# The high half of q copied within SBUF instead of a second evacuation of PSUM

## The chip, the core and the metric

The kernel runs on one core of a Trainium2 chip. The metric is the device time of one execution in microseconds (us), the median of several runs. The engines are TensorE (PE, matmuls; PEld is its weight load), VectorE (DVE), ScalarE (ACT), GpSimd (POOL) and the queue of SyncE (SP), which issues the DMAs.

## The reference

Attention with a bucket mask, then two feed-forward layers. Cut to what matters:

```python
batch, n_heads, seq, head_dim = 2, 8, 768, 64

q_bits = einsum(q, proj) > 0;  k_bits = einsum(k, proj) > 0      # 6 bits each
mask   = bucket(q_bits)[:, None] == bucket(k_bits)[None, :]
scores = where(mask, q @ k.T / sqrt(64), -1e9)
attn   = exp(scores - max(scores)); attn /= sum(attn) + 1e-9
x      = attn @ v                                   # (1536, 512)

h = x @ w_in;   x = (h * tanh(softplus(h))) @ w_out                      # 512 -> 2048 -> 512
h = x @ w_in2;  x = (layernorm(h * softmax(h)) * g_ln) @ w_out2           # 512 -> 1024 -> 512
```

All of it is computed to float32's precision: each factor is split into a high part that TensorE takes exactly and a low rest, and a product is the sum of high times high, high times low and low times high.

## The kernel before

The 16 heads are worked on as 8 pairs. A head has 6 tiles of 128 queries against all 768 keys, so there are 96 tiles. For each tile TensorE makes the scores (line 1238, two operands A and B), VectorE the row maximum (line 1245) and two small steps (lines 1249, 1250), ScalarE the exponential (line 1254). The exponentials are transposed, either as two halves through a DMA (high half by ScalarE, line 1265, low half by GpSimd, line 1287, DMA at line 1290) or by TensorE (line 1273) with halves taken out by ScalarE (line 1277) and VectorE (line 1282). Then TensorE weighs v with them (lines 1305 to 1307), and VectorE divides (lines 1315 to 1319).

Before its tiles, a pair is prepared. GpSimd splits q and k (lines 1137, 1142). TensorE transposes each head's q and k so that the high part lies in 64 partitions and the rest in the other 64 (line 1163, into two PSUM banks called st). ScalarE takes these banks into the operand A (line 1180, 128x768, q scaled by 1/8). The second operand B needs q's high part once more: VectorE reads the same two banks again (line 1171, 64x768, the same scale). k's half of B is copied from A by a DMA (line 1192). Below them, in 12 more rows of B, come the sign bits of q and k (lines 1204, 1212, and the DMA of line 1220), so that one more product adds the mask to the scores.

The first feed-forward layer follows in 48 units of 12 matmuls up (lines 835 to 837) and 12 down (lines 891 to 896), with the function between on ScalarE, VectorE and GpSimd (lines 851 to 877); its weights, 48 chunks, are turned from 64-bit to 32-bit numbers and split on the way (lines 728 to 747). The second layer and its layer norm are 12 tiles at the end (lines 940 to 1029).

Nothing of the order is written out by hand. The class Order holds every step with its engine, its cost in us (COST), its reads and writes, and its due time, which is the number of its tile plus an offset from the table PHASE. Its function run plays the program through with these costs: on each engine it takes, among the steps that can start within 0.1 us of the earliest, the one whose due time is least. What comes out is the order of the instructions on every engine. PSUM's 8 banks and the buffers in SBUF are given out by the same function.

The steps that the change touches have these names there: turn (transposes), evac n h 0 and evac n h 1 (q and k into A), evac n h 2 (q's high part into B). evac="AAAA" gives the first two to ScalarE, again="VV" the third to VectorE for both heads of a pair.

Of the kernel before, what the change touches and what calls it, by code (L numbers as in the profile page):

```python
# [9 lines left out]
F32 = mybir.dt.float32  # L10
# [19 lines left out]


PHASE = dict(
    score=2.89, max=21.69, bias=-20.48, exp=-7.37, hi=37.60, lo=-74.88, tdma=47.79, tr0=9.51, thi0=14.05,
    tlo0=2.17, tr1=10.84, thi1=28.04, tlo1=16.57, weigh=17.46, norm0=29.45, norm1=6.67, norm2=-77.92,
    load=19.06, vload=18.96, split0=-188.88, rest0=28.62, split1=-216.02, rest1=37.27, turn=-44.19,
    evac=-204.06, copy=-27.06, bits0=-103.88, bits1=-136.11, sign=51.37, bdma=40.93, vmax=21.86, vs0=-271.50,
    vs1=9.08, vs2=-210.73, vs3=-129.45, vs4=-56.64, vs5=-127.12, vs6=-290.81, vs7=144.62, vs8=-328.13,
    vh=70.16, vl=45.25, first=63.48, turn_=6.48, evac_=195.41, copy_=-35.91, bits_=94.54, sign_=168.35,
    bdma_=-9.06, vload_=-304.47, vmax_=171.56, vs_=87.04, vh_=-22.87, vl_=-122.68, second=35.58, wload=28.78,
    w0=-41.17, w1=84.02, w2=-26.10, w3=26.15, w4=31.29, w5=19.05, w6=290.37, wpace=-25.50, wat=214.24,  # L40
    wlate=-420.19, turngap=-246.21, x0_=-6.98, x1_=-173.02, x2_=44.49, load_=10.81, const0=66.52,
    begin0=-146.26, vs8_=150.21, outlag=-5.17, up=-162.02, a0=-14.23, a1=40.52, a2=25.54, a3=14.48, a4=30.07,
    a5=-71.43, a6=11.38, a7=-135.40, a8=-17.97, a9=76.71, a10=229.81, da=51.52, db=-112.61, ky0=101.10,
    ky1=110.82, x0=37.16, x1=118.52, x2=72.93, sy0=21.03, sy1=8.66, u2=24.00, n0=-198.44, n1=78.28, n2=130.92,
    n3=-69.22, n4=-178.31, n5=-31.52, n6=140.09, n7=224.60, n8=-279.51, n9=-111.63, n10=-196.61, n11=-61.38,
    n12=-275.68, n13=3.09, t2=-8.41, l0=-92.90, l1=222.42, d2=202.96, ot=-141.26, od=-47.76, wloadL=-156.21,
    w0L=2.89, w1L=23.01, w2L=229.21, w3L=-26.73, w4L=229.00, w5L=-89.36, w6L=-69.41, begin1=-117.25,
    begin2=-102.32, begin3=76.98, const1=123.70, const3=67.06, load0_=-1.00,
)


COST = dict(
    score=0.79, max=0.865, bias=0.18, exp=0.878, hiA=0.733, hiD=0.469, lo=1.61, tr=0.33, thi=0.371, tlo=0.469,
    weigh=0.555, norm0=0.075, norm1=0.106, norm2=0.531, split=0.8, rest=1.79, turn=0.515,
    evacA=0.691, evacV=0.865, warm=3.2, bits=0.7, sign=0.985, vmax=0.87, vs0=0.11, vs1=0.2, vs2=0.11,
    vs=0.07, vs8=0.884, vh=0.733, firstA=0.413, firstD=0.469, w0=0.56, w1=0.602, w2=0.602,
    w3=0.602, w4=0.783, w5=0.52, w6P=1.253, w6D=0.663, x0=0.47, x1=0.478, x2=0.602,
    up=0.7, a0=0.494, a1=0.335, a2=0.602, a3=0.613, a4=0.52, a9=0.52, a10=1.25, da=0.464, db=0.2265,
    sy0=0.52, sy1=0.602, u2=1.39, n0=1.131, n1=1.091, n2=0.069, n3=0.075, n4=1.196, n5=0.069, n6=1.133,
# [17 lines left out]
class Order:  # L77


    def __init__(self, rings, stores, slack, due):  # L80
        self.rings, self.stores, self.slack, self.due = rings, stores, slack, due
        self.kinds = {kind: (name, n) for name, (size, kinds) in stores.items() for kind, n in kinds.items()}
        self.ops, self.index, self.writer, self.readers, self.users = [], {}, {}, {}, {}
        self.spare = dict(e=2, p16=1)

    def op(self, key, engine, cost, base, name, reads=(), writes=(), slot=0, behind=(), wait=()):
        i = len(self.ops)
# [28 lines left out]
    def shared(self, o):  # L116

        key, engine = o[0], o[1]
        if engine == "Pool":
            return True  # L120
        if engine != "DVE":
            return False
        k = key[0]
        if k in ("hi", "sy", "mg"):
            return True
        if k == "first":
            return True
        if k == "w":
            return key[2] == 6
        if k == "n2":  # L130
            return key[3 - 1] == 13
        return False
# [5 lines left out]
    def run(self):  # L138
# [64 lines left out]
        for _ in range(n):  # L203
            best = None
            for e, line in queue.items():
                cand = []
                for r, i in line:
                    r = max(r, free[e])
                    if ops[i][7]:
                        r = ring(i, r)[0]  # L210
                        if r is None:
                            continue
                    cand.append((r, due[i], i))
                if not cand:
                    continue
                first = min(cand)[0]
                pick = min((c for c in cand if c[0] <= first + self.slack), key=lambda c: c[1:])
                if best is None or pick[0] < best[0]:
                    best = (pick[0], e, pick[2])
            at, e, i = best  # L220
            o = ops[i]
            queue[e] = [x for x in queue[e] if x[1] != i]
            for tok, name, m, k in ring(i, at)[1]:
                place[tok] = k
                held[name][k:k + m] = [tok] * m
            for tok in o[7]:
                if tok[0] in taken:
                    taken[tok[0]].append(tok)
            start[i] = at
            if o[8] is not None:  # L230
                hw = max(at + 0.05, hw) + o[2]
                begin = max(hw + 0.65, wire)
                wire = done[i] = begin + o[8]
                if e == "SP":
                    free[e] = begin + 0.85 if o[0][0] in ("tdma", "td") else hw
                else:
                    free[e] = at + 0.05
            else:
                if shared[i]:
                    at = start[i] = max(at, port[other[e]])  # L240
                    port[e] = at + o[2]
                free[e] = done[i] = at + o[2] * (2 if e == "PE" and at < COLD and o[0][0] != "warm" else 1)
            got.append(i)
            for tok in o[10]:
                busy[tok] -= 1
                was = idle.setdefault(tok, {})
                was[frm[i]] = max(was.get(frm[i], 0.0), done[i])
            for j in then[i]:
                left[j] -= 1
                if not left[j]:  # L250
                    queue[ops[j][1]].append((ready(j), j))
# [19 lines left out]
def program_order(pairs, tiles, routes, evac, chunks, wide, due, rings, stores, slack, queues=(), pooled=0,  # L271
# [3 lines left out]
    op = order.op  # L275
# [30 lines left out]
    def prep(n):  # L306
# [6 lines left out]
        for h in range(2):  # L313
            th = t0 if n else h * due["second"]
            for o in range(2):
                sp = ("sp%d" % o, n) if n else ("f", o, h)
                if not n:
                    op(("first", 0, h, o), A, COST["firstA"], th, "first", [(("r%d", "rr%d")[h] % o, 0)], [sp], 0,
                       [("evac", 0, 0, 1)] if h else [])
                    op(("first", 1, h, o), V, COST["firstD"], th, "first", [(("r%d", "rr%d")[h] % o, 0)], [sp])  # L320
                s = ("st", n, h, o)
                d = t0 + (2 * h + o) * due["turngap"] if n else th + 0.01 * o
                op(("turn", n, h, o), T, COST["turn"], d, "turn" + f, [sp, ("ident",)],
                   [s, ("A%d" % o, n, h)])
                e = evac[2 * h + o]
                op(("evac", n, h, o), A if e == "A" else V, COST["evac" + e], d, "evac" + f, [s], [("A%d" % o, n, h)])
                if again and (o if n == 0 else not o):
                    g = again[h]
                    op(("evac", n, h, 2), A if g == "A" else V, COST["evac" + g], d, "evac" + f, [("st", n, h, 0)],
                       [("B", n, h, 0)])  # L330
            for o in range(1 if again else 0, 2):
                dma(("copy", n, h, o), th + 2 * h, "copy" + f, [("A%d" % o, n, h)], [("B", n, h, o)])
            if not n:
                bits(n, (h,), th, f)
# [256 lines left out]
def lsh_attention_moe_kernel(  # L591
# [33 lines left out]
    queues=(),  # L625
    pooled=48,
    split="G",
    again="VV",
    soon=4,
    by_dma=10,  # L630
):
# [533 lines left out]
    def qk_again(p, h):  # L1165
        dst = second(p, h, 0)[0:64].rearrange("p (a n) -> p a n", a=2)
        src = two_banks("st", p, h, 0)[0:64, :, 0:NH]
        if again[h] == "A":
            nc.scalar.activation(dst, src, AF.Copy, scale=SC)
        else:  # L1170
            nc.vector.tensor_scalar(dst, src, SC, None, op0=ALU.mult)
# [244 lines left out]
```

## Time and profile before

| | us |
|---|---|
| median of 3 runs | 654.56 (653.5 to 655.46) |
| profiled execution | 653.04 |
| its span, first to last instruction | 651.3 |
| TensorE busy | 622.2 (96%) |
| VectorE busy | 558.7 (86%) |
| ScalarE busy | 444.0 (68%) |
| GpSimd busy | 367.5 (56%) |

The busy times are sums over the whole span, over stages that have little in common: attention's last weighing matmul is at 247 us, the first layer's last matmul up at 503 us. Matmuls are pipelined and their ends are modelled, so that a busy TensorE is not TensorE at its peak.

### The profile page before, as it was taken

The numbers are of one execution on the slowest core, as the hardware profiler recorded it, in microseconds if no ns is written. First come the engines' busy times: TensorE is split into PE (matmuls) and PEld (weight loads), VectorE is DVE, ScalarE is ACT, GpSimd is POOL, SyncE is SP. The second block draws the span as 40 slices with busy tenths as digits, with TensorE's granted clock in tenths as the row PEclk, the third lists the DMA queues.
The fourth block names the chain that finished last, engine by engine and source line by source line (L and its number), as shares of the span: only waits on it lengthen the run. The fifth ranks groups of instructions, "written<-read, shape, count | busy, mean of one in ns | idle before, by whom it ended". The sixth has DMA issues, their size and how long they took to land.

```text
span 651.3 us, 12308 instructions
## 1 busy us (share of the span) xinstructions
PE 622.2 (96%) x4460; PEld 513.1 (79%) x4460; DVE 558.7 (86%) x1149; ACT 444.0 (68%) x722; POOL 367.5 (56%) x301
## 2 busy tenths in 40 slices
PE   7889999999899899999999999999999999999997
PEld 6668787888778788878888777788788888788885
DVE  4899798898989999999999999999999776675652
ACT  5689897998999986766565566656566545565543
POOL 4678868777765675566666666455476421222210
PEclk9799899999999999999999999999999999999999
DMA  7979978989898892312333322212121022322221
GB/s 203 219 166 148 243 162 159 170 212 166 180 186 165 151 205 76 97 50 79 98 98 97 98 97 66 94 61 70 35 97 34 1 64 45 81 71 81 66 64 49
DMA packets 146909, 73.36 MB, mean 113 GB/s; under 512 B 125344, under 2 KB 139808, under 8 KB 146848
## 3 DMA queue, kind: packets, MB, share of 16 engines
q1 hardware_dynamic: 146848, 72.58, 47.5%
q8 instruction: 35, 0.57, 0.4%
q14 instruction: 26, 0.21, 0.1%
HBM read 34.68 MB, written 3.15 MB: 58 GB/s over the span
## 4 chain that ended last, share of the span: by engine, by line
PE 42%; DVE 22%; ACT 6%; issue 5%; DMA 1%; POOL 0%; DVEq 0%; ACTq 0%; SPq 0%
PE banks L835 4%; PE banks L837 3%; PE banks L940 3%; PE banks L836 3%; PE banks L944 3%; PE banks L941 3%; PE banks L896 3%; PE banks L891 3%; PE banks L892 3%; PE banks L1029 3%; PE banks L1027 3%; DVE mx L1245 3%; PE banks L1028 3%; DVE a L865 2%; DVE a L853 2%
## 5 line engine op out<-in xcount | busy, mean ns | idle before, releaser
L1287 POOL TENSOR_TENSOR store<-store 128x768 f16<-128x768 f32 x64 | 104.9, 1651 | 48.6 <-ACT store L1265 44.3
L1254 ACT ACTIVATE store<-banks,mx 128x768 f32<-128x768 f32 x96 | 92.4, 998 | 12.3 <-DVE mx L1250 5.0
L1245 DVE TENSOR_REDUCE mx<-banks 128x1 f32<-128x768 f32 x96 | 89.4, 946 | 3.1 <-PE banks L1238 2.0
L869 POOL TENSOR_TENSOR n<-c,a 128x512 f32<-128x512 f32 x48 | 63.8, 1329 | 44.6 <-DVE a L865 42.3
L877 POOL TENSOR_TENSOR gl<-n,gh 128x512 fp32r<-128x512 f32 x48 | 62.9, 1310 | 33.4 <-ACT gh L874 33.0
L835 PE MATMUL banks<-xh,w 128*128 128x512 f32 x192 | 76.6, 399 | 2.5 <-DVE a L865 1.6
L891 PE MATMUL banks<-gh,w 128*128 128x512 f32 x192 | 75.8, 395 | 0.9 <-ACT gh L874 0.8
L837 PE MATMUL banks<-xh,w 128*128 128x512 f32 x192 | 75.7, 394 | 0.0
L836 PE MATMUL banks<-xl,w 128*128 128x512 f32 x192 | 75.4, 393 | 0.0
L892 PE MATMUL banks<-gh,w 128*128 128x512 f32 x192 | 75.3, 392 | 0.0
L859 ACT ACTIVATE a<-n,two 128x512 f32<-128x512 f32 x48 | 34.8, 724 | 56.7 <-DVE n L855 56.4
L896 PE MATMUL banks<-gl,w 128*128 128x512 f32 x192 | 72.4, 394 | 0.0
L743 POOL TENSOR_TENSOR w<-wf,w 128x512 fp32r<-128x512 f32 x40 | 51.7, 1293 | 35.2 <-ACT w L741 33.9
L1238 PE MATMUL banks<-A,A 128*128 128x384 f32 x192 | 58.5, 387 | 8.4 <-ACT store L1254 7.4
L1305 PE MATMUL banks<-v,store 128*128 128x65 f16 x576 | 60.0, 193 | 2.3 <-DVE store L1282 1.9
L1306 PE MATMUL banks<-v,store 128*128 128x64 f16 x576 | 59.8, 194 | 0.0
L1307 PE MATMUL banks<-v,store 128*128 128x65 f16 x576 | 59.6, 192 | 0.0
L1305 PEld LDWEIGHTS <-store 128*128 128x128 f16 x576 | 53.0, 96 | 5.0 <-issue 4.6
L1306 PEld LDWEIGHTS <-store 128*128 128x128 f16 x576 | 53.3, 97 | 2.9 <-issue 2.5
L1265 ACT ACTIVATE store<-store 128x768 f16<-128x768 f32 x64 | 53.3, 849 | 0.2
L1307 PEld LDWEIGHTS <-store 128*128 128x128 f16 x576 | 53.5, 99 | 0.0
L1238 PE MATMUL banks<-B 76*128 76x384 f32 x192 | 51.5, 350 | 0.0
(131 smaller groups left out, 1731.7 us busy)
## 6 DMA issues: line engine op xcount, KB each, us to landing
wr<-in_moe_w_in_dram SPq DMA_DIRECT2D x24, 512.0 KB
wr<-in_moe_w_out_dram SPq DMA_DIRECT2D x24, 512.0 KB
vr<-in_v_dram SPq DMA_DIRECT2D x8, 384.0 KB
B<-A SPq DMA_DIRECT2D x16, 192.0 KB
out_dram<-ot SPq DMA_DIRECT2D x12, 256.0 KB
q<-in_q_dram SPq DMA_DIRECT2D x7, 384.0 KB
k<-in_k_dram SPq DMA_DIRECT2D x7, 384.0 KB
B<-bits SPq DMA_DIRECT2D x32, 36.0 KB
```

What stands on the lines that cost most here:

```text
L835: nc.tensor.matmul(h, lhsT=wh[:, ks], rhs=xh, start=(kk == 0), stop=False)
L836: nc.tensor.matmul(h, lhsT=wh[:, ks], rhs=xl, start=False, stop=False)
L837: nc.tensor.matmul(h, lhsT=wl[:, ks], rhs=xh, start=False, stop=(kk == KD - 1))
L891: nc.tensor.matmul(y, lhsT=wh[:, os], rhs=g_t[u][0], start=first, stop=False)
L892: nc.tensor.matmul(y, lhsT=wl[:, os], rhs=g_t[u][0], start=False, stop=False)
L1238: nc.tensor.matmul(s[:, half, 0:NH], lhsT=opnd[nm, p, j, 0][:, cc], rhs=opnd[nm, p, j, 1][:, hs], start=(i == 0), stop=(i == 1),)
L1245: nc.vector.reduce_max(m[:, 1:2], two_banks("s", t)[:, :, 0:NH], axis=AX.XY, negate=True)
L1254: nc.scalar.activation(kept("e", t).rearrange("p (a n) -> p a n", a=2), two_banks("s", t)[:, :, 0:NH], AF.Exp, bias=m[:, 3:4], scale=m[:, ...
L1287: nc.gpsimd.tensor_tensor(p16[:, 1], kept("e", t), p16[:, 0], op=ALU.subtract)
L1305: nc.tensor.matmul(o, lhsT=pt[:, 0, kc, :], rhs=vh, start=(kc == 0), stop=False)
L1306: nc.tensor.matmul(o[:, 0:D], lhsT=pt[:, 0, kc, :], rhs=vl, start=False, stop=False)
L1307: nc.tensor.matmul(o, lhsT=pt[:, 1, kc, :], rhs=vh, start=False, stop=(kc == NC - 1))
```

## The change

Three things change.

The copy. q's high part comes into B from the operand A, which lies in SBUF and already is scaled, and not from PSUM. Of the two heads of a pair one copy is made by ScalarE (kind a), the other by VectorE (kind v). The copy reads what line 1180 has written; it doesn't read the banks.

The scheduler. It gets a table of partners (other): of two steps that read the same bank it starts neither while the other runs. The table is filled where the second copy is of kind A or V. It also gets a set (port) of VectorE steps that it keeps apart from GpSimd's; the copies of kind v are in it. Two costs are added for the copies, 0.733 us on ScalarE and 0.469 on VectorE.

The table PHASE. All its numbers are new, so the whole program is put in another order.

```diff
 PHASE = dict(
-    score=2.89, max=21.69, bias=-20.48, exp=-7.37, hi=37.60, lo=-74.88, tdma=47.79, tr0=9.51, thi0=14.05,
+    score=2.99, max=78.03, bias=-127.69, exp=-377.90, hi=127.72, lo=-75.93, tdma=195.91, tr0=9.77,
...
-    evacA=0.691, evacV=0.865, warm=3.2, bits=0.7, sign=0.985, vmax=0.87, vs0=0.11, vs1=0.2, vs2=0.11,
+    evacA=0.691, evacV=0.865, evaca=0.733, evacv=0.469, warm=3.2, bits=0.7, sign=0.985, vmax=0.87, vs0=0.11, vs1=0.2, vs2=0.11,
...
+        self.other, self.port = {}, set()
...
-        if k in ("hi", "sy", "mg"):
+        if k in ("hi", "sy", "mg") or key in self.port:
             return True
...
+                    k = self.other.get(i)
+                    if k is not None and done[k] is not None:
+                        r = max(r, done[k] + LATENCY[frm[k]].get(e, 0.0))
                     cand.append((r, due[i], i))
...
                     g = again[h]
-                    op(("evac", n, h, 2), A if g == "A" else V, COST["evac" + g], d, "evac" + f, [("st", n, h, 0)],
-                       [("B", n, h, 0)])
+                    op(("evac", n, h, 2), A if g in "Aa" else V, COST["evac" + g], d, "evac" + f,
+                       [("st", n, h, 0) if g in "AV" else ("A0", n, h)], [("B", n, h, 0)])
+                    if g == "v":
+                        order.port.add(("evac", n, h, 2))
+                if again and (o if n == 0 else not o) and g in "AV":
+                    a, b = (order.index["evac", n, h, i] for i in (0, 2))
+                    order.other[a], order.other[b] = b, a
...
-    again="VV",
+    again="av",
...
         src = two_banks("st", p, h, 0)[0:64, :, 0:NH]
-        if again[h] == "A":
+        if again[h] in "av":
+            src = opnd["A", p, h, 0][0:64].bitcast(F32).rearrange("p (a n) -> p a n", a=2)
+            (nc.scalar.copy if again[h] == "a" else nc.vector.tensor_copy)(dst, src)
+        elif again[h] == "A":
             nc.scalar.activation(dst, src, AF.Copy, scale=SC)
```

The numbers of instructions stay the same on TensorE and GpSimd and in the DMAs; VectorE has 16 evacuations less and 8 copies more, ScalarE 8 copies more. In the rows that follow, the changed kernel's line 1180 is the copy and its line 1193 the old line 1180; 1245 has become 1258, 1254 has become 1267, 1265 has become 1278, 1277 has become 1290, 1282 has become 1295, 1128 has become 1138. A_213 and the like are buffers of the operand A; the numbers differ between the programs.

ScalarE at the start of the program, from the evacuations of the first pair's second head to the first tile's exponential, before:

```order
L1180 ACTIVATE A_213<-banks 128x768
L1180 ACTIVATE A_220<-banks 128x768
L728 ACTIVATE wf<-wr 128x512
L1180 ACTIVATE A_259<-banks 128x768
L1180 ACTIVATE A_271<-banks 128x768
L1180 ACTIVATE A_297<-banks 128x768
L1180 ACTIVATE A_306<-banks 128x768
L1128 ACTIVATE v_106<-vr 128x12x64
L1254 ACTIVATE store<-banks,mx_97 128x768
```

and after:

```order
L1180 CAST B<-A_168 64x768
L1193 ACTIVATE A_213<-banks 128x768
L1193 ACTIVATE A_222<-banks 128x768
L738 ACTIVATE wf<-wr 128x512
L1193 ACTIVATE A_252<-banks 128x768
L1193 ACTIVATE A_263<-banks 128x768
L1180 CAST B<-A_263 64x768
L1193 ACTIVATE A_297<-banks 128x768
L1193 ACTIVATE A_309<-banks 128x768
L1267 ACTIVATE store<-banks,mx_97 128x768
```

Two copies have come in ahead of the first exponential, and the copy of the first pair's v has gone behind it.

ScalarE while the fourth pair (p = 3) is prepared, around the exponential of the last tile before it (maximum mx_104), before:

```order
L1180 ACTIVATE A_994<-banks 128x768
L1254 ACTIVATE store<-banks,mx_104 128x768
L1180 ACTIVATE A_1006<-banks 128x768
L1180 ACTIVATE A_1015<-banks 128x768
L1180 ACTIVATE A_1026<-banks 128x768
L1277 ACTIVATE store<-banks 128x384 x2
```

and after:

```order
L1193 ACTIVATE A_1032<-banks 128x768
L1267 ACTIVATE store<-banks,mx_104 128x768
L1290 ACTIVATE store<-banks 128x384
L1193 ACTIVATE A_1095<-banks 128x768
L1290 ACTIVATE store<-banks 128x384
L1193 ACTIVATE A_1125<-banks 128x768
L1290 ACTIVATE store<-banks 128x384
L1180 CAST B<-A_1125 64x768
L1278 ACTIVATE store<-store 128x768
L1267 ACTIVATE store<-banks,mx_97 128x768
```

The evacuations stand with other tiles' work between them now, and the pair's copy comes last.

VectorE at the same place, before:

```order
L1245 TENSOR_REDUCE mx_104<-banks 128x1
L1119 TENSOR_SCALAR pw<-pw 128x1
L1249 TENSOR_SCALAR mx_104<-mx_104 128x1
L1250 TENSOR_SCALAR mx_104<-mx_104 128x1
L1171 TENSOR_SCALAR B<-banks 64x768 x2
L1245 TENSOR_REDUCE mx_97<-banks 128x1
L1282 SCALAR_TENSOR_TENSOR store<-banks,store 128x384
```

and after:

```order
L1258 TENSOR_REDUCE mx_104<-banks 128x1
L744 SCALAR_TENSOR_TENSOR banks<-wr,banks 128x512
L1262 TENSOR_SCALAR mx_104<-mx_104 128x1
L1263 TENSOR_SCALAR mx_104<-mx_104 128x1
L1295 SCALAR_TENSOR_TENSOR store<-banks,store 128x384 x2
L746 SCALAR_TENSOR_TENSOR wf<-wr,banks 128x512
L1180 CAST B<-A_1032 64x768
L1295 SCALAR_TENSOR_TENSOR store<-banks,store 128x384 x2
L1258 TENSOR_REDUCE mx_97<-banks 128x1
```

One copy stands where two evacuations stood, with work for tiles and weights around it.

## Rows read from the trace of the kernel before

**Rows 1.** The page: the span, and each engine's busy us, share and instructions

```profile
span 651.3 us, 12308 instructions
PE 622.2 (96%) x4460; PEld 513.1 (79%) x4460; DVE 558.7 (86%) x1149; ACT 444.0 (68%) x722; POOL 367.5 (56%) x301
```

**Rows 2.** Busy us (instructions) by stretch: length, engines, granted clock, DMA share, GB/s

```profile
core 0: us, PE busy (x) PEld busy (x) DVE busy (x) ACT busy (x) POOL busy (x), PEclk, DMA share, GB/s
...
20.00:60.00 40.00, 34.52 (x298) 28.35 (x297) 34.76 (x88) 32.57 (x45) 33.05 (x24) 0.90 0.81 164
60.00:150.00 90.00, 85.65 (x1116) 74.36 (x1112) 79.06 (x212) 80.89 (x114) 69.50 (x47) 0.98 0.96 185
150.00:190.00 40.00, 35.34 (x439) 29.92 (x437) 34.89 (x84) 35.23 (x51) 29.14 (x20) 1.00 0.92 186
190.00:230.00 40.00, 36.64 (x522) 32.20 (x522) 38.64 (x99) 37.40 (x57) 24.57 (x17) 1.00 0.82 163
...
250.00:504.00 254.00, 250.97 (x1094) 201.11 (x1093) 247.10 (x402) 156.35 (x269) 154.33 (x119) 1.00 0.24 77
504.00:651.30 147.30, 143.16 (x632) 116.72 (x630) 92.67 (x201) 74.56 (x149) 35.21 (x46) 1.00 0.23 58
```

**Rows 3.** Groups by line: count, busy us, mean ns of one, idle before, releasers

```profile
L1287 POOL TENSOR_TENSOR store<-store 128x768 f16<-128x768 f32 x64 | 104.9, 1651 | 48.6 <-ACT store L1265 44.3 <-DVE store L1282 2.2 <-DMA B<-bits 1.0
...
L1265 ACT ACTIVATE store<-store 128x768 f16<-128x768 f32 x64 | 53.3, 849 | 0.2
...
L1171 DVE TENSOR_SCALAR B<-banks 64x768 fp32r<-64x768 f32 x16 | 15.1, 948 | 12.1 <-ACT A L1180 7.6 <-PE banks L1163 2.4 <-DMA B<-bits 2.1
```

**Rows 4.** Waits: engine and line, what it waited for, us in total, times, longest

```profile
DVE B L1171 <- ACT A L1180: 7.6, 7, 2.3
...
ACT A L1180 <- DVE B L1171: 5.2, 8, 1.3
...
ACT A L1180 <- PE banks L1163: 2.9, 4, 1.5
```

**Rows 5.** Timeline of VectorE and ScalarE, 69 to 74 us: start, us, instruction, idle before

```profile
69.13 0.20 DVE L1250 TENSOR_SCALAR mx<-mx 128x1 f32<-128x1 f32 x1
...
70.13 0.95 DVE L1171 TENSOR_SCALAR B<-banks 64x768 fp32r<-64x768 f32 x1 [0.80 <-ACT A L1180]
71.80 0.95 DVE L1171 TENSOR_SCALAR B<-banks 64x768 fp32r<-64x768 f32 x1 [0.72 <-PE banks L1163]
73.63 0.96 DVE L1245 TENSOR_REDUCE mx<-banks 128x1 f32<-128x768 f32 x1 [0.88 <-ACT A L1180]
...
71.12 1.51 ACT L1180 ACTIVATE A<-banks 128x768 fp32r<-128x768 f32 x2 [0.18 <-DVE B L1171]
```

**Rows 6.** Chain of waits while the last pair is prepared: start, us, what

```profile
182.11 0.96 DVE B L1171
...
183.11 0.71 PE banks L1163 x6
...
183.85 0.82 ACT A L1180
...
184.69 0.95 DVE B L1171
```

**Rows 7.** Lines 979 and 1010, SBUF to SBUF: duration ns min/median/max, starts

```profile
L979 DVE TENSOR_SCALAR e<-e,s x12: 810/812/1346, 518.7 to 638.5; 128x1024 f32<-128x1024 f32 x12
...
L1010 POOL COPY e<-wt x20: 761/768/1076, 524.0 to 625.8; 128x512 uint16<-128x512 uint16 x20
L1010 DVE COPY e<-wt x20: 450/458/904, 524.8 to 627.1; 128x512 uint16<-128x512 uint16 x20
```

**Rows 8.** Timeline of ScalarE before the first exponential

```profile
14.46 1.49 ACT L1180 ACTIVATE A<-banks 128x768 fp32r<-128x768 f32 x2
17.09 1.74 ACT L1180 ACTIVATE A<-banks 128x768 fp32r<-128x768 f32 x2 [1.14 <-DVE B L1171]
18.73 0.83 ACT L1128 ACTIVATE v<-vr 128x768 f16<-128x768 f32 x1
```

More of the change, by code (lines that the diff above doesn't have):

```diff
@@ L32 @@
 PHASE = dict(
-    score=2.89, max=21.69, bias=-20.48, exp=-7.37, hi=37.60, lo=-74.88, tdma=47.79, tr0=9.51, thi0=14.05,
[L34 to L47, printed above, removed]
@@ L48 @@
-    begin2=-102.32, begin3=76.98, const1=123.70, const3=67.06, load0_=-1.00,
+    score=2.99, max=78.03, bias=-127.69, exp=-377.90, hi=127.72, lo=-75.93, tdma=195.91, tr0=9.77,
+    thi0=-157.82, tlo0=-43.71, tr1=10.69, thi1=29.74, tlo1=-9.71, weigh=16.88, norm0=17.64, norm1=67.40,
+    norm2=73.69, load=-139.23, vload=27.36, split0=-348.26, rest0=-31.76, split1=-274.92, rest1=-4.35,
+    turn=-271.37, evac=-10.31, copy=-280.20, bits0=-112.56, bits1=-72.95, sign=-224.92, bdma=162.70,
+    vmax=28.12, vs0=-379.90, vs1=44.88, vs2=-178.32, vs3=-4.61, vs4=-196.92, vs5=-118.20, vs6=-172.77,
@@ new lines @@
+    vs7=379.00, vs8=-955.17, vh=217.65, vl=114.36, first=168.17, turn_=607.14, evac_=350.16, copy_=-264.53,
+    bits_=177.32, sign_=-17.00, bdma_=126.57, vload_=-426.86, vmax_=264.98, vs_=330.92, vh_=147.45,
+    vl_=-451.77, second=-56.89, wload=554.52, w0=-556.44, w1=354.50, w2=496.05, w3=-36.46, w4=-148.21,
+    w5=8.83, w6=158.54, wpace=-6.11, wat=177.62, wlate=-215.51, turngap=-465.71, x0_=-15.98, x1_=24.70,
+    x2_=74.58, load_=-186.70, const0=21.80, begin0=-462.28, vs8_=104.01, outlag=-19.71, up=-283.32, a0=-78.68,
@@ new lines @@
+    a1=55.82, a2=354.04, a3=-12.70, a4=-46.38, a5=-116.43, a6=-188.69, a7=-60.07, a8=208.68, a9=87.94,
+    a10=289.34, da=77.98, db=50.26, ky0=132.09, ky1=36.28, x0=39.77, x1=22.02, x2=-13.77, sy0=-182.16,
+    sy1=191.61, u2=39.27, n0=-423.11, n1=-79.54, n2=-7.44, n3=27.30, n4=-275.68, n5=170.60, n6=273.60,
+    n7=-9.59, n8=-307.19, n9=-359.27, n10=-643.40, n11=-226.28, n12=-419.43, n13=220.73, t2=5.96, l0=-259.74,
+    l1=394.15, d2=50.57, ot=-369.94, od=-105.68, wloadL=-772.94, w0L=257.75, w1L=14.27, w2L=118.41,
@@ L49 @@
+    w3L=-50.79, w4L=465.86, w5L=-308.52, w6L=-2.88, begin1=-66.18, begin2=138.50, begin3=181.64, const1=65.32,
+    const3=317.24, load0_=109.71,
 )
```

## The prediction

> **What bounds the kernel now.** I read the busy table first [rows 1], then the busy time of each engine by stretch [rows 2], then the groups and the waits of the lines that the change touches [rows 3, 4], and last one place of the timeline and one of the chain of waits [rows 5, 6].
>
> The table of shares alone would mislead: TensorE is busy 96% of the span, so nothing else would seem to matter. By stretches it falls apart into two regimes [rows 2]. From 250 us on TensorE is busy 250.97 of 254 us and 143.16 of 147.3 us at a granted clock of 1.00. Those 401 us are one queue of matmuls, and the change leaves their number as it is. Whatever is won or lost before 250 us is therefore handed on one for one, up or down.
>
> The attention stretch, 20 to 230 us, is different. Added over its four rows, VectorE is busy 187.35 of 210 us, ScalarE 186.09 and TensorE 192.15, and TensorE's busy time is that of pipelined small matmuls, so it says least. No engine is full over the 210 us. But from 190 to 230 us, where no pair of heads is prepared any more, VectorE is busy 38.64 of 40 us (96.6%) and ScalarE 37.40 (93.5%). From 60 to 190 us, where five pairs are prepared, they are busy 113.95 and 116.12 of 130 us (87.7% and 89.3%). So preparing a pair does not only cost its work, it also opens holes in both engines.
>
> The holes have a name. Line 1180 (ScalarE, q and k out of PSUM, 32 times) and line 1171 (VectorE, the high half of q out of the same two banks, 16 times) never run side by side on a bank. VectorE waited 7.6 us in 7 places for ScalarE's evacuation, and ScalarE 5.2 us in 8 places for VectorE's [rows 4]. At 69 to 74 us the pattern is open to view [rows 5]: VectorE idles 0.80 us, copies, idles 0.72, copies, idles 0.88, and takes its next row maximum only at 73.63 us; it did nothing for the tiles in the 4.3 us from 69.33 (69.13 + 0.20) to there. The chain of waits runs through the same pattern in the last pair: line 1171, transposes, line 1180, line 1171 again [rows 6].
>
> **The change part by part.** The code has three parts: the copy, the scheduler's new rule, and the new table of phases.
>
> *Removed:* 16 VectorE instructions of 948 ns [rows 3], 15.2 us of work. *Added on ScalarE:* 8 copies of 64x768 float32 from SBUF. The nearest row is line 1265, ScalarE from SBUF to SBUF, 768 columns, 849 ns [rows 3]: the same engine, memories and columns, so 8 x 0.849 = 6.8 us. *Added on VectorE:* 8 copies of 64x768 float32 within SBUF. Before has no such row. The copy of 512 short words in SBUF took 458 ns (median), the float32 operation of 1024 columns in SBUF 812 ns [rows 7]; halfway is 635 ns. The ends are 458 ns and the 948 ns of the row removed. I take 635, since 768 columns lie halfway between 512 and 1024: 8 x 0.635 = 5.1 us. VectorE thus loses 10.1 us and ScalarE gains 6.8: the change moves work onto an engine that is as full as the one it relieves.
>
> *The banks.* A head's two banks for q are free after line 1180 alone (0.82 us) and not after 0.82 + 0.95 us [rows 6]. The copy now waits for line 1180's result in SBUF; behind it on VectorE stand row maxima, behind it on ScalarE exponentials. In the place shown in the order, ScalarE has an exponential behind the evacuation of A_1032, and VectorE a row maximum, low halves and a weight step ahead of the copy that reads it; ScalarE's own copy stands behind the pair's last evacuation and one more step. So I cost the new waits at nothing; the cover is the row maxima and low halves ahead of them. If it were gone, the waits of rows 4 would be back, at most 7.6 us.
>
> *The scheduler's rule* fills its table of partners only where the second copy is of kind A or V. Here the kinds are a and v, so the table stays empty and the rule does nothing in this kernel. What remains of the scheduler's part is the entry that makes VectorE's copy count as sharing GpSimd's port, and the two new costs. *The table of phases* reorders the whole program; its effect is read from the order and not from the numbers.
>
> *The start.* Before, ScalarE's evacuations of the second pair stand at 14.46 and 17.09 us with a wait of 1.14 us for VectorE between, then the copy of v, 0.83 us [rows 8]. Now the wait has no cause, a copy (0.85) takes its place, and the copy of v stands behind the sixth exponential: 1.14 - 0.85 + 0.83 = 1.1 us sooner for the first exponential. Against that the second of the two bit transfers for the first tile is issued behind one more transfer on SP; the first exponential does not wait for it as long as ScalarE's own row is the longer one. I take 1.1, with ends 0 and 1.1.
>
> *The attention stretch, by each engine.* Two of ScalarE's copies and two of VectorE's lie before 20 us, with four of the old ones.
> ScalarE: 186.09 + 6 x 0.849 + 0.83 (the copy of v, moved in) = 192.0 us of work. At the 93.5% that it reaches where no pair is prepared, that takes 205.4 us, 4.6 less than 210.
> VectorE: 187.35 - 12 x 0.948 + 6 x 0.635 = 179.8 us; at 96.6% that takes 186.1 us, 23.9 less.
> The slower of the two decides, so ScalarE: 4.6 us. The ends are what ScalarE gives at the share that it has now (88.6%: 216.7 us, 6.7 more) and at VectorE's best share (96.6%: 198.8 us, 11.2 less). I take 93.5% because it is the same stage with the holes gone.
>
> *The later stages* keep their instructions and, by [rows 2], their bound. The place where attention hands over differs a little: 87 of the 96 tiles are weighed before the first matmul of line 835 where 84 were. This moves work from behind that point to ahead of it and adds none; 0.
>
> **Sum.** 1.1 + 4.6 = 5.7 us. The profiled execution took 653.04 us (span 651.3), so 647.3; it lies 1.5 us below the median of 654.56, which makes 648.8 us against that median.
>
> **The rivals.**
> *ScalarE becomes the bound (slower).* For it: the work in the stretch grows by 5.9 us on an engine that is already level with VectorE, and each copy stands ahead of exponentials. If the holes only change their cause (evacuations waiting for transposes, 2.9 us already now [rows 4]) and the share stays at 88.6%, the stretch takes 216.7 us: 6.7 - 1.1 = 5.6 us longer, 660. It decides below a ScalarE share of 192.0 / 211.1 = 90.9%. Against it: 5.2 us of ScalarE's holes were waits for line 1171 and cannot come back.
> *The holes close further.* The lighter VectorE hands out row maxima sooner, ScalarE runs at 96.6%: 11.2 + 1.1 = 12.3 us, 642.3. For it: rows 5 and 6 put both evacuations on the path.
> *VectorE's copies fight GpSimd.* In the tail, copies of both engines run at the same time: VectorE's took 904 ns at most against a median of 458, GpSimd's 1076 against 768 [rows 7]. In the attention stretch GpSimd is busy 156.3 of 210 us (74%), mostly with 1651 ns subtractions [rows 2, 3]. A copy that meets one waits half of it on average: 8 x 0.74 x 0.83 = 4.9 us, and if each ends on a row maximum, the gain shrinks to 0.8: 653.8, no change. At the worst it is 8 x 1.65 = 13.2 us. Against it: VectorE has 19 us of slack over ScalarE by the sums above.
> The Trainium skill (SBUF — State Buffer, section SBUF: two separate sides) says that VectorE in its two-port mode and GpSimd take one shared pair of ports as an exclusive lock for a whole instruction, so that the loser is blocked. By that rule this rival is real for every copy; the trace's 904 and 1346 ns maxima [rows 7] agree in kind, and nothing before shows it at 1651 ns.
> *The new order loses it again.* The table moves everything from 250 us on too. If TensorE's share from 250 to 504 us fell from 98.8% to 97%, its 250.97 us of work would take 258.7, 4.7 us more: 653.5, no change.
>
> **How the numbers follow.** Forecast as summed, 0.45; holes close further, 0.22; GpSimd's port, 0.10; the order loses it, 0.09; ScalarE the bound, 0.14. A measurement of this kernel can tell about 0.3% (2.0 us) from no change. The first two are faster, 0.67; the port and the order fall within 0.3%, and so 0.19; the last is slower, 0.14. The range runs from 642.0, the second case, up to 655.5, where only the further part of ScalarE's case is left out.
>
> **What would show it.** In the profile after, right: the copies and the evacuations of q waiting for each other for under 2 us in all; ScalarE above 93% and VectorE below 92% in the stretch that replaces 20 to 230 us; ScalarE's copies near 850 ns, VectorE's near 635; first exponential near 18.6 us; the later stages as long as before. Wrong: VectorE's copies over 950 ns or spread out (GpSimd), ScalarE below 91% (the slower case), or a difference that arises after 250 us (the order).

## The result

The changed kernel takes 649.18 us (median of 5 runs, 645.77 to 652.12), the kernel before 655.29 us in the 5 runs beside them. The ratio is 0.990, with a 95% interval of 0.986 to 0.994. Timed again later, the changed kernel took 648.71 us (6 runs) against 655.46, ratio 0.988 (0.985 to 0.991). So it is 6 to 7 us faster, and the forecast of 648.8 us, with its range of 642.0 to 655.5, holds. Most of the reasoning that led to the size does not, as the experiments show; that the sum came out is in good part luck.

Two profiled executions of the changed kernel are used below: the first took 652.12 us (the slowest of its runs, span 650.3), the later one 647.95 (span 646.2). Where a number could be an accident of one execution, both are given. Of the runs reported below, those more than 1.5% above the fastest of their kernel (one each of e6, e9 and e11, two of before) count in the medians but not in the ratios and clock figures; without them the medians are 683.2 us for e6, 660.7 for e9 and 649.3 for e11.

The page of the first, lines as in [rows 1]:

```profile
span 650.3 us, 12264 instructions
...
PE 622.4 (96%) x4460; PEld 516.8 (79%) x4460; DVE 552.9 (85%) x1141; ACT 448.1 (69%) x730; POOL 369.1 (57%) x301
```

VectorE is busy 5.8 us less and ScalarE 4.1 more; TensorE's 622 us are the same. The busy time by stretch, columns as in [rows 2]:

```profile
20.00:60.00 40.00, 34.69 (x264) 29.64 (x263) 33.00 (x88) 31.84 (x44) 31.61 (x23) 0.82 0.81 173
60.00:150.00 90.00, 85.89 (x1175) 75.10 (x1173) 78.15 (x207) 82.53 (x119) 70.59 (x48) 1.00 0.92 187
150.00:190.00 40.00, 36.71 (x449) 31.45 (x449) 35.61 (x88) 38.60 (x56) 29.28 (x20) 1.00 0.81 169
190.00:230.00 40.00, 37.19 (x540) 32.87 (x541) 37.61 (x97) 38.04 (x59) 25.97 (x18) 1.00 0.78 162
...
250.00:504.00 254.00, 250.25 (x1081) 201.16 (x1080) 245.01 (x398) 154.62 (x267) 153.21 (x118) 0.99 0.24 77
```

Against [rows 2], ScalarE is fuller where pairs are prepared (121.13 us of the 130 from 60 to 190, 116.12 before), and VectorE about as full as it was (113.76; 113.95 before).

What the second step of a head's q meant to the others is best read from what waited for it. First the removed line in the kernel before (durations in ns as min/median/max, then why its engine idled ahead of it, then who idled for it):

```profile
L1171 DVE TENSOR_SCALAR B<-banks x16: 934/950/951, 7.2 to 184.7; 64x768 fp32r<-64x768 f32 x16
...
its engine sat idle before it (us, times) until:
  ACT A L1180: 7.6, 7
  PE banks L1163: 2.4, 4
  DMA B<-bits: 2.1, 1
who waited for it (us, times):
  ACT A L1180: 5.2, 8
...
  PE banks L1163: 1.7, 3
  PE banks L1204: 1.5, 2
...
  PE banks L1238: 0.3, 1
...
```

and the copies that stand for it in the changed kernel:

```profile
L1180 ACT CAST B<-A x8: 823/835/884, 8.7 to 183.0; 64x768 fp32r<-64x768 f32 x8
L1180 DVE CAST B<-A x8: 536/564/1472, 11.2 to 181.4; 64x768 fp32r<-64x768 f32 x8
...
its engine sat idle before it (us, times) until:
  ACT A L1193: 4.2, 3
who waited for it (us, times):
busy tenths in 40 slices 1000101000000000000000000000000000000000
```

The last list is empty: no idle time of any engine is put down to a copy (a wait for several things is put down to the one that came last). Before, the evacuation itself kept ScalarE waiting 5.2 us, and TensorE's matmuls 1.7 + 1.5 + 0.3 = 3.5 us for banks that it held. Of the waits ahead of the step, 4.2 of 7.6 us are left, in three places, now for ScalarE's result.

How much of that reaches the end is read at the handover. The first matmul of the weighing, by its line, with the first and last start in the kernel before, in the changed kernel, and in its later execution (span 646.2):

```profile
L1305 PE MATMUL banks<-v,store x576: 190/193/208, 43.7 to 246.9; 128*128 128x65 f16 x192
```

```profile
L1318 PE MATMUL banks<-v,store x576: 190/193/207, 45.1 to 244.7; 128*128 128x65 f16 x192
```

```profile
L1318 PE MATMUL banks<-v,store x576: 190/193/206, 43.7 to 242.0; 128*128 128x65 f16 x192
```

The last weighing starts 2.2 and 4.9 us sooner. From there to the end of the span it is 651.3 - 246.9 = 404.4 us before, 405.6 and 404.2 after. So the later execution hands its 4.9 us on in full. The first loses 1.2 us of its 2.2. Its timeline of TensorE behind the handover (start, duration, instruction, idle time before it):

```profile
251.88 0.66 PE L825 MATMUL banks<-cs,xn 128*128 128x128 f32 x4 [1.40 <-DVE xl L834]
...
257.86 0.66 PE L825 MATMUL banks<-cs,xn 128*128 128x128 f32 x4 [1.05 <-DVE wf L746]
259.10 0.50 PE L901 MATMUL banks<-gh,w 128*128 128x512 f32 x1 [0.58 <-DVE xl L834]
...
259.92 0.63 PE L845 MATMUL banks<-xh,w 128*128 128x512 f32 x1
260.34 0.63 PE L846 MATMUL banks<-xl,w 128*128 128x512 f32 x1
```

and the same place in the later execution:

```profile
255.15 0.66 PE L825 MATMUL banks<-cs,xn 128*128 128x128 f32 x4 [1.05 <-DVE wf L746]
256.39 0.50 PE L901 MATMUL banks<-gh,w 128*128 128x512 f32 x1 [0.58 <-DVE xl L834]
...
257.19 0.40 PE L845 MATMUL banks<-xh,w 128*128 128x512 f32 x1
257.43 0.39 PE L846 MATMUL banks<-xl,w 128*128 128x512 f32 x1
```

Both executions have the same three waits, 1.40, 1.05 and 0.58 us within 8 us, so these are not what differs. Behind them the first has eight matmuls that start about 0.42 us apart instead of 0.23, some 1.6 us in all: the granted clock is 0.51 from 259.80 to 263.20 us, its lower level (1.2 GHz), and 1.00 at the same place of the later execution.

### The profile page after: what moved, and what is told of

Read it like the earlier page. It is cut to its first block, busy times and chain, and to the rows that moved or that the text cites. A ratio compares the mean times of both kernels' runs of the same rounds, so it can differ in the third digit from the quotient of the medians.

```text
span 650.3 us, 12264 instructions
## 1 busy us (share of the span) xinstructions
PE 622.4 (96%) x4460; PEld 516.8 (79%) x4460; DVE 552.9 (85%) x1141; ACT 448.1 (69%) x730; POOL 369.1 (57%) x301
## 4 chain that ended last, share of the span: by engine, by line
PE 61%; DVE 9%; ACT 2%; issue 2%; DVEq 0%; ACTq 0%
PE banks L901 6%; PE banks L902 6%; PE banks L906 6%; PE banks L845 6%; PE banks L847 6%; PE banks L846 6%; PE banks L1039 3%; PE banks L951 3%; PE banks L1037 3%; PE banks L954 3%; PE banks L950 3%; PE banks L1038 3%; DVE mx L1258 2%; DVE store L1295 1%; ACT store L1267 1%
## 5 line engine op out<-in xcount | busy, mean ns | idle before, releaser
L906 PE MATMUL banks<-gl,w 128*128 128x512 f32 x192 | 70.3, 393 | 0.0
## 6 DMA issues: line engine op xcount, KB each, us to landing
B<-A SPq DMA_DIRECT2D x16, 192.0 KB
```

Source lines behind the costliest of these rows:

```text
L906: nc.tensor.matmul(y, lhsT=wh[:, os], rhs=g_t[u][1], start=False, stop=last)
```

## The experiments

All numbers are medians of the runs of one kernel; before stood at 654.9 to 655.5 us beside them. A run's time goes with the granted clock that it had: over all these runs, each kernel against its own mean, by 3.5 us for 0.01 of mean clock. The table therefore has a second column, the mean time shifted by that slope to a clock of 0.989. Where an edit itself lowers the clock, the shift hides a part of its price; so both columns are read.

| kernel | order of the program | second part of q | median us | at clock 0.989 |
|---|---|---|---|---|
| before | old | PSUM, VectorE x16 | 655.1 | 654.8 |
| e2 | old | copy, both engines | 653.4 | 653.8 |
| e11 | old | 12 of 16 left out | 650.2 | 650.7 |
| e9 | new | PSUM, VectorE x16 | 662.0 | 659.9 |
| changed kernel, e1 | new | copy, both engines | 649.2, 648.7 | 648.7, 648.7 |
| e10 | new | 12 of 16 left out | 650.3 | 649.5 |
| e3 | new | copy, VectorE x16 | 653.9 | 652.3 |
| e4 | new | copy, ScalarE x16 | 654.2 | 653.1 |
| e8 | new | copy, VectorE x8, DMA x8 | 653.9 | 651.2 |
| e7 | new, x turned later | copy, both engines | 649.2 | 649.6 |
| e12 | planned anew, true costs | copy, both engines | 669.2 | 664.5 |
| e5 | planned anew, new table | PSUM, VectorE x16 | 676.8 | 669.7 |
| e6 | planned anew, old table | copy, both engines | 684.2 | 675.6 |

"New order" is the changed kernel's, row for row; "planned anew" means that the planner made another order.

### The changed kernel once more (e1)

No edit; it is the second measurement and the second profile named above.

> The changed kernel itself once more, as the standard for the runs beside it, and for a second profile. All theories: 649 us, between 646 and 652. If the handover hole (TensorE idle 4 to 5 us between 244 and 260 us) belongs to the order it is there again; if it was chance, it is gone. The half-speed clock between 20 and 56 us, some 14 us long in the first profile, may differ.

Measured: 648.71 us (647.53 to 650.59), ratio 0.988. The gain is there again, and the profile shows the spread between executions of one kernel: the last weighing starts 2.7 us sooner than in the first.

### The copy alone (e2)

```
-        src = two_banks("st", p, h, 0)[0:64, :, 0:NH]
-        ...
+        src = opnd["A", p, h, 0][0:64].bitcast(F32).rearrange("p (a n) -> p a n", a=2)
+        (nc.scalar.copy if "av"[h] == "a" else nc.vector.tensor_copy)(dst, src)
```

in the order of before; where the step stood ahead of the evacuation that it now reads, it goes right behind it.

> The kernel before with its own table and its own order; only the 16 second evacuations are copies within SBUF, ScalarE for a pair's first head and VectorE for its second. A copy that stood ahead of its evacuation in the order is put right behind it. Theory banks (the gain is the end of the turn-taking on PSUM banks, less ScalarE's 8 x 0.84 us): 648 to 651, 4 to 7 us under the kernel before. Rival table (the gain is the new order, and the copy only moves work to a full ScalarE): 654 to 658, no gain or a loss.

Measured: 653.36 us, ratio 0.996 (0.993 to 0.999). That lies between the two expectations: the new copy in the old place brings 1 to 2 us of the 6. Its line in the profiled execution (657.41 us):

```profile
L1168 ACT CAST B<-A x8: 832/835/839, 6.6 to 189.3; 64x768 fp32r<-64x768 f32 x8
L1168 DVE CAST B<-A x8: 537/552/1468, 12.1 to 187.2; 64x768 fp32r<-64x768 f32 x8
...
its engine sat idle before it (us, times) until:
  ACT A L1177: 12.4, 7
who waited for it (us, times):
...
```

Nobody waits for the copy here either. But the old order puts it where VectorE has to wait for ScalarE's evacuation, 12.4 us in 7 places, against 7.6 us in [rows 4] and 4.2 us in the new order (this profile is of the slowest of its twelve runs, so its times are on the long side): the old place suits a step that shares the banks, not one that needs the result.

### All copies on one engine (e3, e4)

```
-            (nc.scalar.copy if again[h] == "a" else nc.vector.tensor_copy)(dst, src)
+            nc.vector.tensor_copy(dst, src)
```

and, for e4, `nc.scalar.copy(dst, src)`, both in the new order.

> The changed kernel in its exact order, but all 16 copies on VectorE. ScalarE loses 8 x 0.835 = 6.7 us of work, VectorE gains 8 x 0.564 = 4.5. Theory ScalarE decides the attention stretch: 3 to 6 us under the changed kernel, about 644 to 646. Rival VectorE or GpSimd's port decides: 0 to 5 us over it, 649 to 654, with VectorE's copies often near the 1472 ns that one of eight took.

> The changed kernel in its exact order, but all 16 copies on ScalarE: 8 x 0.835 = 6.7 us more on ScalarE, 4.5 us less on VectorE. Theory ScalarE decides: 4 to 7 us over the changed kernel, 653 to 656. Rival VectorE decides: 0 to 4 us under it, 645 to 649.

Measured: 653.87 us (ratio 0.996, 0.993 to 0.998) and 654.24 us (0.997, 0.995 to 1.000), 5 us above the changed kernel each, 4 at equal clock. e3 takes 8 x 0.84 = 6.7 us off ScalarE, puts 14.8 - 6.8 = 8.0 us on VectorE and is slower, as its rival said; e4, the other way round, is as much slower, as the theory of ScalarE said. Each alone would have confirmed one engine. Together they say that neither decides alone, and that the order has room for about seven more microseconds on neither engine.

e3's copies in its profiled execution:

```profile
L1180 DVE CAST B<-A x16: 544/772/1880, 8.6 to 187.5; 64x768 fp32r<-64x768 f32 x16
```

### ScalarE's copies by DMA (e8)

```
+            if again[h] == "a":
+                by("copy").dma_start(out=second(p, h, 0)[0:64].bitcast(F32), in_=opnd["A", p, h, 0][0:64].bitcast(F32))
+            else:
+                nc.vector.tensor_copy(dst, src)
```

> The changed kernel in its order, but ScalarE's 8 copies made by DMAs on SP's queue at the same places; VectorE keeps its 8. ScalarE loses 6.7 us of work and nobody else's compute grows. Theory ScalarE's load decides the attention stretch: 3 to 6 us under the changed kernel. Rival what counts is the place of the work and not the load: within 1.5 us of it; or slower by 1 to 4 us, if SP's queue then stands behind the evacuations and holds up the transposing DMAs.

Measured: 653.90 us, ratio 0.999 (0.996 to 1.002). ScalarE loses its eight copies to SP's queue, VectorE keeps its own, and the kernel gains nothing. Its runs had a mean clock of 0.982, the changed kernel's 0.988; at equal clock 2.5 us are left of the 5 us that it lies above the changed kernel, and whether the lower clock is a consequence of the edit or an accident stays open. The last rival of the expectation is not excluded: in the profile ScalarE waits 3.8 us in 4 places for transposing DMAs (store<-store), 0.3 us in one place in the changed kernel. So e8 shows no gain from 6.7 us less on ScalarE, but it doesn't show the load alone; e10 does that better.

### No copies (e10) and no second evacuations (e11)

```
     def qk_again(p, h):
+        if p > 1:
+            return second(p, h, 0)
```

with four buffers of its own for the operand B, in the new order (e10) and in that of before (e11).

> The changed kernel's order with 12 of the 16 copies left out (only the first four, one for each of the four buffers, are made; the other twelve pairs of scores use an older high part of q, so this is no result of attention). It takes 6 x 0.83 = 5.0 us off ScalarE and 6 x 0.77 = 4.6 us off VectorE, and nothing else changes. If either engine's work in the attention stretch sets the time, as predicted, it gains 4 to 5 us on the changed kernel: 644 to 645 us. If what is left of the copies lies beside other work, it stands within 1.5 us of 649.

> The order of before with 12 of the 16 second evacuations left out (the same twelve; only the first four are made). It takes 12 x 0.948 = 11.4 us off VectorE, and with them the waits for the bank that the two engines took in turn. By the prediction's theory, in which a gain of 5.7 us follows from sixteen of them at a price in ScalarE's copies, this gains at least 12/16 x (5.7 + 4.6 - 1.1) = 6.9 us: 648 us or less. If the order holds the time, and the copy alone in it brought 1 to 2 us, this too gains no more than 2 to 3: 652 to 653 us.

Measured: e10 650.31 us, ratio to before 0.992 (0.989 to 0.995), not below the changed kernel, as its second expectation said; e11 650.24 us, ratio 0.994 (0.990 to 0.998), between its two expectations.

This pair shows what the step is worth. In the order of before, the 12 evacuations together cost 4 to 5 us of time for their 11.4 us of work; how much of that is the work and how much the hold on the banks, e11 doesn't separate, since it takes both away. In the new order the 12 copies cost nothing that can be measured, and the changed kernel stands at the time that either order reaches without them, about 650 us. So there is nothing more to win from the step that these runs could tell. That handing out B's four buffers in another way costs nothing by itself was not run. What holds the kernel at 650 us is not shown either; in e10's profile the time set free turns up as waits: VectorE's low halves out of the transposes wait 10.4 us for ScalarE's high halves, 5.3 in the changed kernel, and ScalarE's exponentials 5.8 us for VectorE's maxima, 2.3 there. The new order's last weighing without the copies starts where the changed kernel's does in the execution of the same length (both 652.12 us); below it that of e11 (span 647.3):

```profile
L1323 PE MATMUL banks<-v,store x576: 190/193/277, 43.1 to 244.5; 128*128 128x65 f16 x192
L1310 PE MATMUL banks<-v,store x576: 190/193/262, 44.1 to 242.5; 128*128 128x65 f16 x192
```

### The new order with the old work (e9)

```
-        if again[h] in "av":
-            ...
+        if "VV"[h] == "A":
             nc.scalar.activation(dst, src, AF.Copy, scale=SC)
         else:
             nc.vector.tensor_scalar(dst, src, SC, None, op0=ALU.mult)
```

> The changed kernel's order, row for row, with the old work in it: all sixteen second parts are read from PSUM by VectorE, as before the change (a part goes ahead of its place only where a bank is written again in between: 7 of 16). VectorE gets about 16 x 0.95 - 6.2 = 9.0 us more work than in the changed kernel, ScalarE 6.7 us less. If the work taken from VectorE is what was won, this stands at the time of before, 655 us, or above. If the new order by itself won the time and the kind of copy is beside the point, it stands at 649 to 650 us. If an order serves only the durations that it was made for, it stands between or above both, 652 to 658 us.

Measured: 661.98 us, ratio 1.011 (1.007 to 1.014). That is the first expectation, the time of before or above, and 11 to 13 us above the changed kernel, more than the 9.0 us of VectorE's work that the edit adds. The new order is therefore not better by itself. It rests on the banks being free after the first evacuation. Its line (profiled execution 660.07 us):

```profile
L1181 DVE TENSOR_SCALAR B<-banks x16: 935/940/951, 7.2 to 191.2; 64x768 fp32r<-64x768 f32 x16
...
its engine sat idle before it (us, times) until:
  ACT A L1190: 5.1, 4
who waited for it (us, times):
...
  PE banks L1214: 6.6, 5
...
  PE banks L1248: 5.0, 4
...
  PE banks L1173: 2.3, 3
...
```

TensorE's bit products (1214), scores (1248) and transposes (1173) wait 6.6 + 5.0 + 2.3 = 13.9 us for the step, in 12 places; in the kernel before they waited 3.5 us in 6, as shown above. The matmuls stand where the copy leaves a bank free and the evacuation does not. The sixteen steps of 0.95 us cost 4 to 5 us (for twelve, e11) in the order made for them, and 11 to 13 in the other.

Against e3, e9 separates the hold from the work. Both have all sixteen steps on VectorE in the new order, 14.8 us of copies in e3 and 15.0 us of evacuations in e9 (7 of them moved ahead), and nothing else differs. e9 takes 7 to 8 us more (7.6 at equal clock), and in e3 no wait is put down to the step. In the new order that much is the price of reading the banks, and not of VectorE's time. The last weighing starts 5 us later (e3, span 653.3, then e9, span 658.3):

```profile
L1318 PE MATMUL banks<-v,store x576: 190/193/278, 42.1 to 249.2; 128*128 128x65 f16 x192
L1315 PE MATMUL banks<-v,store x576: 190/193/281, 43.4 to 254.2; 128*128 128x65 f16 x192
```

### The planner (e5, e6, e12) and the turns of x (e7)

e5 is the changed kernel with `again="VV"`, so that the planner's rule for engines that share banks is in force and the old work is done; e6 is the changed code with the table of phases of before; e12 changes two costs:

```
-    evacA=0.691, evacV=0.865, evaca=0.733, evacv=0.469,
+    evacA=0.691, evacV=0.865, evaca=0.835, evacv=0.564,
```

> The changed kernel's table and scheduler, but the second evacuation from PSUM on VectorE for both heads as before; its table of partners is filled, so the scheduler lets the two engines take turns on a bank. In the runs so far the copies alone in the old order gave 2.1 us (at equal clock 1.1) of the 6.5 us. Theory the table brings the rest by itself: 649 to 652. Rival the table and the copies only work together: 653 to 658.

> The changed kernel's code, copies and scheduler, but the numbers of the old table, so that the scheduler plans the copies with the old due times. Theory an order that knows of the copies is what counts, whatever the table: 648 to 651. Rival the new table's order is what counts: 652 to 655, as with the copies alone in the old order.

> The changed kernel with one line of the planner's costs altered: a copy by ScalarE counts 0.835 us in place of 0.733 and one by VectorE 0.564 in place of 0.469, which are the durations that the trace of the changed kernel has. The work is the same; the planner makes a new order of it from the same due times. If the work on the engines sets the time, it stands within 2 us of 649. If the table of due times and the costs belong together number for number, so that any order planned anew from this table is a bad one, it stands 10 to 30 us above, as the two kernels did in which the table and the costs didn't belong together (677 and 684 us), and then those two say nothing of the copies.

Measured: 676.78 us (ratio 1.033, 1.029 to 1.036), 684.17 us (1.043, 1.038 to 1.047) and 669.17 us (1.020, 1.015 to 1.024). e12 does the changed kernel's work, with costs nearer to the trace, and is 20 us slower. Its last weighing (profiled execution 669.86 us, span 668.1):

```profile
L1318 PE MATMUL banks<-v,store x576: 190/193/278, 33.3 to 257.0; 128*128 128x65 f16 x192
```

Against the first execution of the changed kernel, 12.3 us of its loss arise ahead of the handover and 5.5 behind it (668.1 - 257.0 = 411.1 us against 405.6). e5 and e6 met neither of their expectations. Every order that was planned anew, with this table or the old one, is 20 to 35 us worse than the changed kernel (16 to 27 at equal clock), and so e5 and e6 say nothing of the copy, nor of the planner's rule: what they show is that table, costs and kinds belong together. The worth of the rule stays open; in the changed kernel it has no step to work on.

e7 lets the turns of x for the first late matmuls be due later (x0 from 39.77 to 60, x1 from 22.02 to 42.25, x2 from -13.77 to 6.46), to close the waits behind 250 us.

> The changed kernel with three due times of the new table raised by 20.2 (x0, x1, x2: the transposes of the attention's result for the second and third block of rows). All instructions up to 248 us stand as in the changed kernel; of the 32 transposes that follow one another there, the last 16 go some units later. TensorE idled 4.5 us between 248 and 260 us in two profiles of the changed kernel, behind VectorE's low parts of these transposes. Theory the hole is on the path: 2 to 4 us under the changed kernel, 645 to 647. Rival the later units are bound by VectorE's total work, which is the same: within 1 us of it.

Measured: 649.21 us, ratio 0.992 (0.988 to 0.995): no change against the changed kernel, as the rival said. The idle time that the expectation puts at 4.5 us is 1.40 + 1.05 + 0.58 = 3.0 us in both profiles; in e7's only the 1.40 us are left, and nothing is gained.

## Why the prediction was right, point by point

**The stretches: right.** The attention stretch decides and the rest passes it on. From the last weighing to the end it is 404.4 us before, 404.2 and 405.6 in the two executions of the changed kernel, 404.1 in e9 (658.3 - 254.2), 405.8 in e10, and 404.8 in e11 (647.3 - 242.5). Over 12 us of difference at the handover it moves by 1.7 at most; only in the orders planned anew is it longer (411.1 us in e12). "The later stages: 0" was a fair term, with the clock's 1.2 us as its error.

**Removed and added work: right in size.** ScalarE's copies were put at 849 ns and took 835. VectorE's were put at 635 ns; the median is 564, the sum of the eight 6.8 us in the first profile and 6.2 in the second, against 5.1 predicted. The difference is the third rival, below. The net on the pages is smaller than the forecast's: VectorE's busy time falls by 5.8 us and not by 10.1, ScalarE's rises by 4.1 and not by 6.8; what makes up the rest was not followed.

**The banks: right in kind, and the real cause.** Nothing waits for a copy, where ScalarE and TensorE waited for the evacuation. The forecast took this for the condition of the gain ("the holes gone") and went on to compute the gain from ScalarE's share. The pair e10 and e11 shows what went away: a step that cost 4 to 5 us for 12 of the 16, replaced by one that costs nothing measurable. That its hold on the banks matters more than VectorE's time is shown in the new order (e9 against e3, 7 to 8 us at equal work); for the old order it is argued from the waits, 5.2 us of ScalarE and 3.5 of TensorE. The new waits, which the forecast cost at nothing, are 4.2 us on VectorE in three places, not under 2; no one else's wait is put down to the copy.

**The planner's rule: as read,** without a step to work on. **The table of phases:** the forecast read its effect from the order and gave it no term of its own. That was the largest gap. The copy in the old order brings 1 to 2 us, the new order with the old work loses 5 to 7 against before, and only both together win 6.

**The start: wrong.** 1.1 us were expected, the first exponential at 18.6 us. It starts at 19.3 and 20.2 us in the two executions; before, it started at 19.8. Two executions of one kernel differ by 0.9 us there, and nothing of the term can be seen.

**ScalarE decides, 4.6 us: wrong.** This is the step that failed; that its number lay near the result is luck. ScalarE is busy 191.0 and 194.4 us from 20 to 230 us, where the forecast put 192.0 us of work into 205.4, and its share is 91.0% and 92.6%, not above 93%. (VectorE's, 87.8% and 89.0%, is below 92% as forecast.) Taking 5.0 us off ScalarE and 4.6 off VectorE gains nothing (e10), nor does taking 6.7 off ScalarE alone, though there VectorE (e3) or SP's queue (e8) got the work, while 7 to 8 more on either engine cost about 4 at equal clock (e3, e4). An engine whose work can be lowered without a gain does not set the time, even if raising it costs. At 91% the forecast had put the turn to "slower"; the first execution sits there and is faster. A share of 93.5% that an engine reaches in one stage was no measure of what another stage is worth.

The sum should have priced the step itself: 16 of them, each with its wait for the bank, its work and its hold on others. The forecast had the rows for it, 7.6 + 5.2 us of waits and 15.2 us of work; that about 6 us of these reach the end, no row of before could say.

**The rivals.** *ScalarE becomes the bound*: no; its eight copies have no price at their places, though eight more have (e4). *The holes close further*: no; e10 shows a floor at about 650 us with the step gone. *VectorE's copies fight GpSimd*: the fight is there. Two of the eight copies in the changed kernel, VectorE first, GpSimd beside it:

```profile
73.97 1.20 DVE L1180 CAST B<-A 64x768 fp32r<-64x768 f32 x1
...
101.22 1.47 DVE L1180 CAST B<-A 64x768 fp32r<-64x768 f32 x1 [1.68 <-ACT A L1193]
```

```profile
73.10 1.66 POOL L1300 TENSOR_TENSOR store<-store 128x768 f16<-128x768 f32 x1 [0.54 <-ACT store L1278]
...
100.63 1.65 POOL L1300 TENSOR_TENSOR store<-store 128x768 f16<-128x768 f32 x1 [0.19 <-ACT store L1278]
```

GpSimd's subtractions end at 74.76 and 102.28 us, the copies at 75.17 and 102.69, 0.41 us later both times: the copy gets through when the subtraction is over. That agrees with the rule of the Trainium skill (SBUF — State Buffer, section SBUF: two separate sides) which the forecast named, an exclusive hold for a whole instruction. (The 0.41 us are less than the 0.54 of a free copy, so a part of the copy's time had passed by then; which, the trace doesn't show.) But three copies of eight lost time to a long GpSimd operation, 2.3 us in all (6.77 - 8 x 0.56), not 4.9, and by e10 those lie beside other work. In e3, where all sixteen run on VectorE, the port takes 14.8 - 16 x 0.55 = 6.0 us, and part of e3's loss is likely that; the share was not separated. *The new order loses it again*: no, from 250 to 504 us TensorE is busy 250.25 of 254 us, 250.97 before.

## What to carry to other kernels

Ask who waits for a step before asking which engine does it: a step that holds a shared buffer costs through those who want the buffer, and a copy that nobody waits for can cost nothing on engines that are 90% busy. Leave the step out, in the old order and in the new, before summing shares: two runs give its price and what is left to win. In a kernel whose order is fitted to its durations, a step and its place are one change; swapped alone, the same step gained 1 to 2 us, its order alone lost 5 to 7, both together gained 6.

## What the runs showed of the hardware

A float32 copy of 64x768 within SBUF takes VectorE 0.54 to 0.57 us when it runs free, and up to 1.88 us when it meets a long GpSimd operation. The hold goes both ways: in e3, with twice as many copies on VectorE, GpSimd's subtraction of line 1300 (1287 before), 1639 to 1670 ns in the changed kernel, took up to 1974 (one of 1.97 us began at 75.64 us, beside a copy from 74.77 to 76.10):

```profile
L1300 POOL TENSOR_TENSOR store<-store x64: 1632/1650/1974, 22.1 to 238.2; 128x768 f16<-128x768 f32 x64
```

ScalarE's copy of the same size is slower when free (0.82 to 0.88 us) but kept its duration in every kernel that has it.

The time of one kernel moved with the granted clock by more than the change is worth: the runs of before beside the last four kernels (e9 to e12) go from 650.3 us at a mean clock of 0.994 to 661.3 at 0.973. A single pair of runs could have shown this change with either sign.
